# Three head pairs with float32 PV instead of four, scaled weight parts on a third engine, and an order planned with other durations

## The chip, the cores and the metric

The kernel runs on one core of a Trainium2 chip. The metric is the device time of one execution in microseconds (us), lower is better. Engines are named as the profile names them: PE (matrix products), PEld (its weight loads, which overlap PE), DVE, ACT and POOL (element-wise work), SP (the queue that issues most DMAs). The kernel is one program: each engine has its own list of instructions in a fixed order, and they wait for each other by semaphores.

## The reference, cut

Three layers over a batch of 4, 576 positions, 8 heads of 64 columns (model width 512), all float32:

```python
scores = (q @ k.T) / 8                       # per batch and head, 576 x 576
thresh = max(scores, axis=-1) - tau
attn   = exp(where(scores >= thresh, scores, -1e9) - max(scores))
x = (attn / sum(attn)) @ v                   # heads side by side: 576 x 512
x = x + relu(layernorm(x) * g @ w_ch1) @ w_ch2            # hidden width 2048
theta = x @ w_theta
y = w_tok_r @ (x * cos(theta)) + w_tok_i @ (x * sin(theta))
u = x + y
out = u + relu(u @ w_ch)
```

The kernel gives float32 accuracy from 16-bit matrix products by splitting each operand into a high and a low fp16 part and adding three products.

## The kernel before, in words

**Attention** goes by batch `b`, by tile `t` of 128 query rows (four full tiles and one tail of 64 rows per batch) and by head pair `hp` (0 to 3): one call of `couple(b, t, hp)` (L900) makes two units, one per head (the tail makes one). A unit's scores `S` are a product of 64 contraction rows (L930); DVE takes the row maximum and copies to `ringE` (`top`, L1037), ACT masks (L1053). From here there are two ways:

- *Whole* (`turned`, L992; pairs in `WHOLE`, L37: all four head pairs of batch 0): PE turns the masked scores with five float32 transposes per unit (`tm` L1008, `tl` L1009), ACT takes the exponential from PSUM (L1013, and L1021 for the tails of the pair), and the product with V (`pv`, L945) is float32. V is loaded as it is (`vraw`, L790) and nothing is split.
- *Split* (the end of `unit`, L1026, for all other pairs): ACT takes the exponential in place (L1079), `hi16` copies to fp16 on ACT, DVE or POOL (L305, L307 or L309), `lo16` and `lo16t` subtract on DVE or POOL (L318), and an SP DMA transposes the 16-bit tile (`PT<-ringP`, L1100). The product (L953 for batches 0 and 1, L958 for 2 and 3) has 14 fp16 instructions per unit and head. V needs its own split: a sum of squares on ACT (L813), one small product on PE (`pvs`, L820), scale steps, a high part on ACT (L838), a low part on DVE or POOL (L842 or L845).

**The first channel layer** goes by groups of three tiles (`ln_group`, L1160): layer norm, then per chunk of 128 hidden columns 12 products of 384 columns (`p_A`, L713) and 9 of 512 (`chA`, L736). Chunks 0 to 11 are made in three `Quad`s of eight weight pieces while attention runs; batch 0 has no such work until its first three tiles are done.

**Weights** arrive as 64-bit words (pairs of 32-bit) and `cvt` (L474) turns each piece into two fp16 parts: absolute value `s1` on ACT or DVE (L500, L502), low words `s1b` on ACT (L507), three DVE steps `s2a`, `s2b`, `s2c` (L511, L518, L523), an integer sum `s3` on POOL (L528), the scaled high part `s4` on ACT (L533) and the scaled low part `s5` on DVE (L539).

**The end**: `mix` (`y`, L1876) and `chan` (`o`, L1934) per batch; `chan`'s last steps per block of 128 output columns are two ACT halves (L1951), two DVE halves (L1958) and one output DMA (L1963).

**The order** is planned when the program is built. Every step is given to `Plan.op` with the engines that may do it and a duration in ns for each. `Plan.play` simulates the list of free engines: at each turn the step that can start first is placed, on the engine that would end it first. PE breaks ties by a key (attention before layer work), the others by the latest time at which the step may end, which `Plan.latest` works out backwards from the pass before. `LAT` stands for the way from one engine to another, `DMA_LAT` for a transfer's landing. `Plan.run` makes eight passes, keeps the ranks of the shortest and plays it for real. Where the plan leaves PE idle over 200 ns, `keep` (L460) puts in filling products (`warm<-one`, L466); the program starts with 20 products on ones (`warmup`, L458).

Of the kernel before, what the change touches and what calls it, by code (L numbers as in the profile page):

```python
# [22 lines left out]
KB = 4  # L23
# [12 lines left out]
WARM = 20  # L36
WHOLE = ((0, 0), (0, 1), (0, 2), (0, 3))  # L37
TRT = 580.0
PVT = 2250.0
# [15 lines left out]
LAT = 300.0  # L55
# [8 lines left out]
DMA_LAT = 2600.0  # L64
# [29 lines left out]
OFF = {"ln": -20000.0, "lnev": -10000.0, "cvt1": 0.0, "top": -500.0, "mask": -500.0, "exp": -5000.0, "thr": -2500.0, "hi16": 500.0, "lo16": -1500.0, "evict": -4000.0, "guard": -3000.0, "att": -1500.0, "prep": 0.0, "ev": -2500.0, "fill": -3000.0, "cvt": 6000.0, "late": LATE}  # L94

# [19 lines left out]
class Op:  # L115
    __slots__ = ("kind", "start", "pen", "fn", "engs", "deps", "acq", "rel", "key", "off", "grow", "first", "rank", "prev", "left", "users",
                 "ready", "fin", "eng")


class Plan:  # L120
# [5 lines left out]
    def op(self, fn, deps=(), acq=(), rel=(), key=0.0, kind="fill", pen=None, **engs):  # L126
        o = Op()
        o.pen = pen or {}
# [22 lines left out]
    def run(self, passes=8):  # L151
# [8 lines left out]
        best = rank = None  # L160
        for k in range(passes + 1):
            for res, was in free.items():
                res.free[:] = was
                res.last = {}
            for sl, n in uses:
                sl.uses, sl.i, sl.end = n, None, 0.0
            if k == passes:
                for o, r in zip(self.ops, best[1]):
                    o.rank = r
            span = self.play(k == passes)  # L170
            if k == passes:
# [28 lines left out]
    def play(self, real):  # L200
# [9 lines left out]
        while left:  # L210
# [40 lines left out]
            o.fin = clock[e] + (DMA_LAT if e == "Q" else 0.0)  # L251
# [25 lines left out]
def tile_kernel(  # L277
# [169 lines left out]
    k_load = op(c_load, A=100, kind="att")  # L447
# [26 lines left out]
    def cvt(src, shape, hi, lo, name, start=(), acq=(), kind="cvt", peak=None, late=None, early=False):  # L474
# [56 lines left out]
        def s4(e):  # L531
            if late:
                A.activation(out=hi(), in_=st["w"], func=AF.Copy, scale=late())  # L533
# [3 lines left out]
        def s5(e):  # L537
            if late:
                V.scalar_tensor_tensor(out=lo(), in0=st["w"], scalar=late(), in1=hi(), op0=ALU.mult, op1=ALU.subtract)  # L539
            else:  # L540
# [5 lines left out]
        ob = op(s1b, [o], A=ac(n), **kw)  # L546
# [318 lines left out]
    class Queries:  # L865


        def __init__(self, b, t, prev):
# [6 lines left out]
            def load_f(e):  # L875
                q["f"] = ap.tile([128, 4, 128], F32, tag=str(self.sl), name="qf_" + nm)
                Q.dma_start(q["f"], qT[b, :, :, c0:c0 + 128].rearrange("h p c -> p h c"))
# [15 lines left out]
            if b in QF:  # L893
                self.ready = [op(load_f, prev, (self.sl,), Q=1000, kind=kd)]
# [1023 lines left out]
    def chan(b):  # L1918
# [3 lines left out]
        for c in range(KB):  # L1922
# [15 lines left out]
            o = None  # L1938
            for kk in range(KB):
                o = op(mm(kk), [o, d["c"][kk], cw_ops[kk]] + pz_ops[b // 2][1:], sl if kk == 0 else (), T=6 * mh_(288),  # L1940
                       key=key + 0.01 * c)

            o_pre = o.deps[0]
# [22 lines left out]
            oa = [op(relu_(n), [o, o_p], (), (sl[n],), A=ap_(288), kind="ev") for n in range(2)]  # L1966
# [3 lines left out]
            op(out, oa, (), (sn,), Q=820)  # L1970
# [90 lines left out]
```

## Time and profile before

| what | us |
|---|---|
| median of 3 runs (lowest to highest) | 808.51 (808.27 to 809.12) |
| the profiled execution | 808.34 |
| its span, first to last instruction | 806.2 |
| PE busy in the span | 798.3 |
| DVE / ACT / POOL busy | 634.5 / 533.6 / 395.2 |

All rows are of that one execution. Times in rows count from the span's start. The duration of one PE instruction includes its way through the array, so consecutive products overlap: what a group occupies is read from its start to the start of the next group.

### The profile page before, as it was taken

How to read it: one execution, taken by the hardware profiler on the slowest of the kernel's cores; microseconds unless marked ns; L12 is line 12 of the kernel's file. 1: busy time of each engine (PE TensorE's matmuls, PEld its weight loads, DVE VectorE, ACT ScalarE, POOL GpSimd, SP SyncE). 2: the span in 40 equal slices, each digit the busy share in tenths (PEclk: the TensorE clock that was granted, in tenths of full speed). 3: DMA queues.
4: the chain of work that ended last, by engine and by line, in shares of the span. 5: the costliest groups of instructions: out<-in, count | busy, mean ns of one | idle time of the engine just before them, and what ended most of it. 6: DMA issues, size and time to landing. Idle time of an engine off the chain costs nothing.

```text
span 806.2 us, 16608 instructions
## 1 busy us (share of the span) xinstructions
PE 798.3 (99%) x6243; PEld 529.7 (66%) x6243; DVE 634.5 (79%) x1305; ACT 533.6 (66%) x980; POOL 395.2 (49%) x470
## 2 busy tenths in 40 slices
PE   9999999999999999999999999999999999999997
PEld 8888866665566677666655555555545777567775
DVE  4879799999789788888867777777668995698843
ACT  5899999997678788788835354455557461474612
POOL 1332478778577557687832122212354480545611
PEclk9999999999999999999999999999999999999999
DMA  8334598967387998968982532673374105010011
GB/s 230 136 101 137 180 201 185 214 143 126 108 160 158 155 199 175 218 124 147 159 209 115 173 98 76 236 244 131 89 173 140 32 21 105 1 60 1 16 45 59
DMA packets 194351, 106.40 MB, mean 132 GB/s; under 512 B 157408, under 2 KB 175328, under 8 KB 194272
## 3 DMA queue, kind: packets, MB, share of 16 engines
q1 hardware_dynamic: 193984, 105.34, 54.7%
q8 instruction: 49, 0.80, 0.4%
q14 instruction: 30, 0.25, 0.1%
q10 hardware_dynamic: 288, 0.00, 0.0%
HBM read 52.50 MB, written 15.73 MB: 85 GB/s over the span
## 4 chain that ended last, share of the span: by engine, by line
PE 92%; ACT 3%; DVE 2%; issue 1%; DMA 1%; POOL 0%; DVEq 0%; POOLq 0%
PE p_A L713 17%; PE chA L736 16%; PE y L1876 13%; PE S L930 9%; PE p_B L713 6%; PE c L736 6%; PE th L1712 5%; PE o L1934 5%; PE pv L945 4%; PE pv L958 4%; PE tm L1008 2%; PE pv L953 2%; PE warm L458 1%; DMA vraw<-in_v 1%; PE th_t L1712 1%
## 5 line engine op out<-in xcount | busy, mean ns | idle before, releaser
L713 PEld LDWEIGHTS <-w 128*128 128x128 f16 x1152 | 109.5, 98 | 78.0 <-issue 4.5
L736 PE MATMUL chA<-w,hbuf 128*128 128x512 f16 x648 | 149.5, 379 | 0.0
L713 PE MATMUL p_A<-ringX,w 128*128 128x384 f16 x864 | 148.7, 326 | 0.1
L736 PEld LDWEIGHTS <-hbuf 128*128 128x128 f16 x864 | 81.3, 98 | 92.0 <-issue 4.0
L1037 DVE TENSOR_SCALAR_CACHE_REDUCE ringE<-S,ncoef 128x576 f32<-128x576 f32 x144 | 112.7, 811 | 24.2 <-PE S L930 21.1
L318 POOL TENSOR_TENSOR ringP<-ringE,ringP 128x512 f16<-128x512 f32 (+2 forms) x118 | 123.0, 1056 | 13.5 <-ACT ringP L305 8.6
L1053 ACT ACTIVATE ringE<-ringE,tiny 128x576 f32<-128x576 f32 x144 | 105.6, 771 | 2.1 <-POOL tiny L1045 1.2
L1876 PE MATMUL y<-tok,z 128*128 128x288 f16 x768 | 97.4, 286 | 0.0
L1876 PEld LDWEIGHTS <-z 128*128 128x128 f16 x768 | 75.1, 98 | 19.4
L1079 ACT ACTIVATE ringE<-ringE,ntaup 128x576 f32<-128x576 f32 x108 | 78.4, 764 | 0.1
L309 POOL TENSOR_SCALAR ringP<-ringE 128x576 f16<-128x576 f32 x64 | 47.7, 748 | 41.1 <-ACT ringE L1079 39.3
L719 ACT ACTIVATE hbuf<-p_A 128x384 f16<-128x384 f32 x72 | 34.9, 485 | 49.4 <-PE p_A L713 48.9
L722 DVE SCALAR_TENSOR_TENSOR hbuf<-p_A,hbuf 128x384 f16<-128x384 f32 x72 | 39.3, 551 | 17.8 <-ACT hbuf L719 17.5
L1298 DVE SCALAR_TENSOR_TENSOR x<-chA,qs,x 128x512 f32<-128x512 f32 x54 | 40.0, 745 | 14.9 <-PE chA L736 13.6
L736 PE MATMUL c<-w,hbuf 128*128 128x512 f16 x216 | 50.7, 379 | 0.0
L713 PE MATMUL p_B<-ringX,w 128*128 128x384 f16 x288 | 50.6, 326 | 0.0
L930 PE MATMUL S<-kf,qf 64*128 64x288 f32 (+1 forms) x288 | 50.0, 426 | 0.1
L1934 PE MATMUL o<-x1T,cw 128*128 128x288 f16 x384 | 47.7, 286 | 0.0
L1934 PEld LDWEIGHTS <-cw 128*128 128x128 f16 x384 | 37.6, 98 | 9.7
L1712 PE MATMUL th<-th,x1T 128*128 128x512 f16 x192 | 42.6, 379 | 0.0
L313 ACT ACTIVATE x1T<-u,cs 128x576 f16<-128x576 f32 x16 | 12.3, 770 | 45.6 <-DVE u L1903 40.9
L528 POOL TENSOR_TENSOR raw_w<-raw_w 128x512 int32<-128x512 int32 x20 | 21.3, 1068 | 41.4 <-DVE raw_w L523 16.8
(243 smaller groups left out, 1568.9 us busy)
## 6 DMA issues: line engine op xcount, KB each, us to landing
raw_w<-in_w SPq DMA_DIRECT2D x20, 512.0 KB, 5.0
rawe<-in_w SPq DMA_DIRECT2D x12, 512.0 KB, 5.1
raw_tok<-in_wtok SPq DMA_DIRECT2D x12, 432.0 KB, 4.2
xscr<-x SPq DMA_DIRECT2D x18, 256.0 KB, 3.4
xl<-xscr SPq DMA_DIRECT2D x18, 256.0 KB, 4.9
out<-uo SPq DMA_DIRECT2D x16, 288.0 KB, 2.1
vraw<-in_v SPq DMA_DIRECT2D x12, 320.0 KB, 3.7
scr<-ringX SPq DMA_DIRECT2D x5, 768.0 KB, 5.0
```

What stands on the lines that cost most here:

```text
L309: G.tensor_scalar(out=out, in0=in_, scalar1=1.0, scalar2=0.0, op0=ALU.mult, op1=ALU.add)
L318: e.tensor_tensor(out=out, in0=a, in1=b, op=ALU.subtract)
L713: T.matmul(st["ps"][:, :n], lhsT=ch.w1(a, c), rhs=xt()[:, c, bb, :n], start=(kk == 0), stop=(kk == 11))
L736: T.matmul(ps, lhsT=h[:, a, t * 128:(t + 1) * 128], rhs=ch.w2(bb), start=(first and (a, bb) == M2[0]), stop=(stop and (a, bb) == M2[2]))
L930: T.matmul(w["S"][:, n, 0:288], lhsT=qd.q[a][r, hp], rhs=d.k[c][r, n * 288:(n + 1) * 288], start=(k == 0), stop=(k == len(seq) - 1))
L1037: V.tensor_scalar(out=st["e"].rearrange("p (a k) -> p a k", a=2), in0=st["S"][:, :, 0:288], scalar1=ncoef, scalar2=None, op0=ALU.mult, op1 ...
L1053: A.activation(out=st["e"], in_=st["e"], func=AF.Prelu, bias=cp["thr"][:, j:j + 1], scale=-1.0, alpha=STEEP)
L1079: A.activation(out=e_of(ws), in_=e_of(ws), func=AF.Exp, bias=ntaup, scale=1.0)
L1298: V.scalar_tensor_tensor(out=x[p, t0 + t], in0=st["ch", t], scalar=chunks[i].quad.inv, in1=x[p, t0 + t], op0=ALU.mult, op1=ALU.add)
L1712: T.matmul(st["ps"], lhsT=src(a, c), rhs=w[:, c * 512:(c + 1) * 512], start=(kk == 0), stop=(kk == 11))
L1876: T.matmul(st["ps"][n][:, 0:288], lhsT=a, rhs=w[:, n * 288:(n + 1) * 288], start=(k == 0 and q == 0), stop=(k == 8 and q == 2))
L1934: T.matmul(st["ps"][n][:, 0:288], lhsT=w[:, cs], rhs=d["t"][a][:, kk, n * 288:(n + 1) * 288], start=(kk == 0 and q == 0), stop=(kk == 3 an ...
```

## The change

1. `WHOLE` loses (0, 3): the fourth head pair of batch 0 goes the split way, with fp16 PV.
2. `s1b`, `s4` and `s5` of a weight piece may also go to POOL (`s5` as two instructions there).
3. The plan looks each step's duration up in a table `DUR` by engine, step and old duration; `LAT` is 180 instead of 300, `DMA_LAT` 2700 instead of 2600; `run` takes the fourth pass instead of the best of eight.
4. The start: 11 warming products instead of 20; the first queries' load is issued from ACT's queue instead of SP's.
5. The end: in the last block of the last batch the two column halves are computed one after the other and each has an output DMA of its own.

```diff
-WARM = 20
-WHOLE = ((0, 0), (0, 1), (0, 2), (0, 3))
+WARM = 11
+WHOLE = ((0, 0), (0, 1), (0, 2))
+S5G = 2000.0
-LAT = 300.0
+LAT = 180.0
-DMA_LAT = 2600.0
+DMA_LAT = 2700.0
+PICK = 3
+DUR = {
+    "T": {
...
+        "couple.pv": {850: 829, 950: 846, 2250: 2181},
+        "turned.tr": {580: 551},
+        "warmup": {4000: 6007},
...
+    "A": {
+        "cvt.s4": {550: 601, 617: 682},
+        "unit.expo.go": {760: 704},
+        "unit.mask": {760: 691},
...
-    def op(self, fn, deps=(), acq=(), rel=(), key=0.0, kind="fill", pen=None, **engs):
+    def op(self, fn, deps=(), acq=(), rel=(), key=0.0, kind="fill", pen=None, lat=0.0, **engs):
...
+        name = fn.__qualname__.replace("tile_kernel.<locals>.", "").replace("<locals>.", "")
+        engs = {e: DUR.get(e, {}).get(name, {}).get(round(ns), ns) for e, ns in engs.items()}
...
-    def run(self, passes=8):
+    def run(self):
...
-        for k in range(passes + 1):
+        rank = None
+        for k in range(PICK + 1):
...
-            span = self.play(k == passes)
-            if k == passes:
-                break
-            if best is None or span < best[0]:
-                best = span, [o.rank for o in self.ops]
+            span = self.play(k == PICK)
...
-    k_load = op(c_load, A=100, kind="att")
+    k_load = op(c_load, A=900, kind="att")
...
         def s1b(e):
             rw = st["rw"]
-            A.activation(out=rw[:, :, 0], in_=rw[:, :, 0].bitcast(U32), func=AF.Copy, scale=2.0 ** -29)
+            if e is A:
+                A.activation(out=rw[:, :, 0], in_=rw[:, :, 0].bitcast(U32), func=AF.Copy, scale=2.0 ** -29)
+            else:
+                G.tensor_scalar(out=rw[:, :, 0], in0=rw[:, :, 0].bitcast(U32), scalar1=2.0 ** -29, scalar2=0.0, op0=ALU.mult,
+                                op1=ALU.add)
...
+                    G.tensor_scalar(out=hi(), in0=st["w"], scalar1=late(), scalar2=0.0, op0=ALU.mult, op1=ALU.add)
...
+            elif late:
+                G.tensor_scalar(out=st["w"], in0=st["w"], scalar1=late(), scalar2=0.0, op0=ALU.mult, op1=ALU.add)
+                sub(G, lo(), st["w"], hi())
...
-        ob = op(s1b, [o], A=ac(n), **kw)
+        ob = op(s1b, [o], A=ac(n), G=CHG[1], **kw)
...
-            o_ = op(s4, [o] + deps, A=ac(n), **kw)
+            o_ = op(s4, [o] + deps, A=ac(n), G=CHG[1], **kw)
             if late:
-                return op(s5, [o_], (), [sl], V=vc(n, V2), **kw)
+                return op(s5, [o_], (), [sl], V=vc(n, V2), G=S5G, **kw)
...
-                self.ready = [op(load_f, prev, (self.sl,), Q=1000, kind=kd)]
+                self.ready = [op(load_f, prev, (self.sl,), Q=1000, kind=kd) if queries else
+                              op(load_f, (), (self.sl,), A=450, lat=3200.0, kind="guard")]
...
+            final = (b, c) == (B - 1, KB - 1)
...
+            if final:
+                for n in range(2):
+                    for kk in range(KB):
+                        o = op(mm1(kk, n), [o, d["c"][kk], cw_ops[kk]] + pz_ops[b // 2][1:], (sl[n],) if kk == 0 else (),
+                               T=3 * mh_(288), key=key + 0.01 * c)
+                    by_n.append(o)
...
+                        Q.dma_start(outT[b, c * 128:(c + 1) * 128, ns], st["u"][:, 0, ns])
```

## Rows read from the trace of the kernel before

**Rows 1.** The page, section 1: busy time, share of the span, instructions.

```profile
PE 798.3 (99%) x6243; PEld 529.7 (66%) x6243; DVE 634.5 (79%) x1305; ACT 533.6 (66%) x980; POOL 395.2 (49%) x470
```

**Rows 2.** What PE waited for: total us, times, longest us.

```profile
PE pvs L820 <- ACT va L813: 1.3, 2, 1.1
```

**Rows 3.** Filling products, lines by form, before 97 us and whole (times, busy, mean).

```profile
L466 PE MATMUL warm<-one 128*128 128x256 bf16 x37 | 5.9, 274 | 0.0
...
L466 PE MATMUL warm<-one 128*128 128x256 bf16 x52 | 7.9, 274 | 0.0
```

**Rows 4.** Two stretches: stretch, its us, PE, PEld, DVE, ACT, POOL busy, clock, DMA.

```profile
14.00:97.00 83.00, 82.75 (x699) 72.46 (x698) 68.53 (x180) 77.67 (x152) 26.86 (x35) 1.00 0.49 148
110.00:200.00 90.00, 89.61 (x844) 54.99 (x842) 88.54 (x193) 80.91 (x151) 73.25 (x82) 1.00 0.85 165
```

**Rows 5.** Timeline of PE, whole way: start, length, instruction; full pair, then tail.

```profile
76.33 0.66 PE L1008 MATMUL tm<-ident,ringE 128*128 128x128 f32 x4
...
76.93 1.00 PE L945 MATMUL pv<-vraw,PT 128*128 128x65 f32 x8
...
79.11 0.17 PE L611 MATMUL pw_w<-tiny,one 128*128 128x1 bf16 x1
...
94.20 0.68 PE L945 MATMUL pv<-vraw,PT 128*64 128x65 f32 x8
...
95.42 0.63 PE L945 MATMUL pv<-vraw,PT 128*64 128x65 f32 x8
```

**Rows 6.** Timeline of PE, split way of batch 1: one full pair, and what follows.

```profile
129.68 1.01 PE L953 MATMUL pv<-va,PT 128*128 128x65 f16 x28
130.52 0.81 PE L736 MATMUL chA<-w,hbuf 128*128 128x512 f16 x3
```

**Rows 7.** The start: timelines of PE to 4.98 and 8.5 us, of SP's queue.

```profile
0.98 4.27 PE L458 MATMUL warm<-ones 128*128 128x128 f32 x23 [0.98 <-POOL ones L424]
...
7.29 1.24 PE L930 MATMUL S<-kf,qf 64*128 64x288 f32 x8
...
0.72 0.40 SPq L757 DMA_DIRECT2D kf<-in_kT  x1
1.18 0.43 SPq L877 DMA_DIRECT2D qf<-in_qT  x1
```

**Rows 8.** Landing of the first query load, in us after its issue.

```profile
DMA to landing us min/median/max: 5.0/5.0/5.0
```

**Rows 9.** The end: timeline of ACT and DVE after 800 us.

```profile
801.39 0.89 ACT L1951 ACTIVATE uo<-o,cs 128x288 f32<-128x288 f32 x2 [2.13 <-PE o L1934]
801.98 0.95 DVE L1958 SCALAR_TENSOR_TENSOR uo<-uo,cs 128x288 f32<-128x288 f32 x2 [2.08 <-issue]
```

**Rows 10.** Lines by form, whole span: the split way's steps on POOL and ACT.

```profile
L318 POOL TENSOR_TENSOR ringP<-ringE,ringP 128x512 f16<-128x512 f32 x78 | 98.0, 1261 | 6.5 <-ACT ringP L305 4.2
L309 POOL TENSOR_SCALAR ringP<-ringE 128x576 f16<-128x576 f32 x64 | 47.7, 748 | 41.1 <-ACT ringE L1079 39.3
L318 POOL TENSOR_TENSOR ringP<-ringE,ringP 128x128 f16<-128x128 f32 x33 | 23.5, 712 | 6.6 <-ACT ringP L305 4.0 <-DVE ringP L307 2.0
...
L1079 ACT ACTIVATE ringE<-ringE,ntaup 128x576 f32<-128x576 f32 x108 | 78.4, 764 | 0.1
```

**Rows 11.** Lines by form, 0 to 97 us: weight pieces on ACT and DVE.

```profile
L533 ACT ACTIVATE w<-raw_w,qs 128x512 f16<-128x512 f32 x8 | 5.9, 795 | 0.0
...
L539 DVE SCALAR_TENSOR_TENSOR w<-raw_w,qs,w 128x512 f16<-128x512 f32 x8 | 6.2, 801 | 0.6 <-ACT w L533 0.6
L518 DVE TENSOR_SCALAR a_w<-a_w 128x512 uint32<-128x512 uint32 x14 | 6.2, 442 | 0.1
L523 DVE SCALAR_TENSOR_TENSOR rawe<-rawe,a_w 128x512 uint32<-128x512 uint32 x6 | 4.1, 676 | 0.0
```

**Rows 12.** Two DVE lines, 100 to 200 us: ns shortest/median/longest, first and last start.

```profile
L518 DVE TENSOR_SCALAR a_w<-a_w x10: 408/737/1376, 108.0 to 196.3; 128x512 uint32<-128x512 uint32 x10
...
L523 DVE SCALAR_TENSOR_TENSOR rawe<-rawe,a_w x6: 683/978/1173, 112.8 to 197.3; 128x512 uint32<-128x512 uint32 x6
```

More of the change, by code (lines that the diff above doesn't have):

```diff
@@ L250, in play @@
             before, clock[e] = clock[e], s + o.engs[e]
-            o.fin = clock[e] + (DMA_LAT if e == "Q" else 0.0)
+            o.fin = clock[e] + (DMA_LAT if e == "Q" else o.lat)
             o.eng, o.start = e, s
@@ L532, in s4 @@
             if late:
-                A.activation(out=hi(), in_=st["w"], func=AF.Copy, scale=late())
+                if e is A:
+                    A.activation(out=hi(), in_=st["w"], func=AF.Copy, scale=late())
+                else:
+                    G.tensor_scalar(out=hi(), in0=st["w"], scalar1=late(), scalar2=0.0, op0=ALU.mult, op1=ALU.add)
             else:
@@ L537, in s5 @@
         def s5(e):
-            if late:
+            if late and e is V:
                 V.scalar_tensor_tensor(out=lo(), in0=st["w"], scalar=late(), in1=hi(), op0=ALU.mult, op1=ALU.subtract)
+            elif late:
+                G.tensor_scalar(out=st["w"], in0=st["w"], scalar1=late(), scalar2=0.0, op0=ALU.mult, op1=ALU.add)
+                sub(G, lo(), st["w"], hi())
             else:
@@ L1936, in mm, with mm1, go @@
                 return go
[L1938 to L1943, printed above, removed]
+            final = (b, c) == (B - 1, KB - 1)
+            def mm1(kk, n, c=c, sl=sl, st=st):
+                def go(e):
+                    if kk == 0:
+                        st.setdefault("ps", []).append(m_tile(sl[n], [128, 512], f"o_{b}_{c}_{n}"))
+                    cs = slice(kk * 512 + c * 128, kk * 512 + (c + 1) * 128)
+                    for q, (w, a) in enumerate(((cw(0), 0), (cw(0), 1), (cw(1), 0))):
+                        T.matmul(st["ps"][n][:, 0:288], lhsT=w[:, cs], rhs=d["t"][a][:, kk, n * 288:(n + 1) * 288],
+                                 start=(kk == 0 and q == 0), stop=(kk == 3 and q == 2))
+                return go
+            o, by_n = None, []
+            if final:
[4 more added lines that the diff above has]
+                    by_n.append(o)
+            else:
+                for kk in range(KB):
+                    o = op(mm(kk), [o, d["c"][kk], cw_ops[kk]] + pz_ops[b // 2][1:], sl if kk == 0 else (), T=6 * mh_(288),
+                           key=key + 0.01 * c)
+                by_n = [o, o]
+            o_pre = by_n[0].deps[0]
             def pre(e, c=c, st=st, sn=sn):
@@ L1965, in chan @@
             o_p = op(pre, [o_pre, d["c"][c]], [sn], V=vc(576, V2), G=gc(576), kind="ev")
-            oa = [op(relu_(n), [o, o_p], (), (sl[n],), A=ap_(288), kind="ev") for n in range(2)]
+            oa = [op(relu_(n), [by_n[n], o_p], (), (sl[n],), A=ap_(288), kind="ev") for n in range(2)]
             oa = [op(fin_(n), [oa[n]], V=vc(288), kind="ev") for n in range(2)]
@@ L1969, in chan, with half, go @@
             ends.append(o_p)
-            op(out, oa, (), (sn,), Q=820)
+            if final:
+                sn.uses = 2
+                def half(n, c=c, st=st):
+                    def go(e):
+                        ns = slice(n * 288, (n + 1) * 288)
+                        Q.dma_start(outT[b, c * 128:(c + 1) * 128, ns], st["u"][:, 0, ns])
+                    return go
+                for n in range(2):
+                    op(half(n), [oa[n]], (), (sn,), Q=820)
+            else:
+                op(out, oa, (), (sn,), Q=820)
         op(lambda e: None, ends, (), (d["sl"],), C=0)
```

163 lines of the change are left out of this document (156 added, 7 removed).

## The prediction

> **What bounds the kernel now.** The page comes first: PE is busy for 798.3 of 806.2 us [rows 1]. Busy PE may hide waits, so I read next who PE waited for: the longest entry is 1.3 us in all [rows 2]. The timeline shows that groups follow each other without gaps, so PE's own work sets the end almost everywhere. Two parts of that work are useless: the warming products, which occupy the time from 0.98 us to the first scores at 7.29 us with two fills [rows 7], and the fills, 52 in all, 37 of them before 97 us [rows 3]. Their busy time of 5.9 and 7.9 us [rows 3] includes the way through the array; by 256 columns at 2.4 GHz (the granted clock is 1.00 [rows 4]) a fill occupies 0.11 us, an estimate: 37 are 4.1 us, 52 are 5.7 us.
>
> Then the stretches [rows 4]. From 14 to 97 us, while batch 0's attention runs alone, the other engines have room: DVE 68.5, ACT 77.7 and POOL 26.9 us of 83 each, together 173.1 of 249, or 70%. From 110 to 200 us, with layer work beside attention, they have little: 88.5, 80.9 and 73.3 of 90 each, 90% together, and DVE is at 98%. A reader should keep both in mind: a microsecond taken off PE is worth a microsecond only as long as these three keep up.
>
> The sums below go against the profiled execution, 808.34 us (span 806.2 and 2.1 around it); the median of the runs is 808.51.
>
> **The fourth head pair on the split way.** Removed on PE for a full pair: two units of transposes, 0.60 us each (76.33 to 76.93), and the float32 product, 2.18 us (76.93 to 79.11) [rows 5]: 3.38 us. Added: 28 fp16 products in 0.84 us (129.68 to 130.52) [rows 6]. Scores are the same. That is 2.5 us per pair and four full pairs: 10.2 us. The tail pair loses 0.60 and 1.22 us (94.20 to 95.42) [rows 5] and gains about 0.9: 0.9 us saved. Together 11.1 us less. PE gets one more `pvs` product, and in an in-order engine its wait for ACT's sum of squares can show: it cost up to 1.1 us once [rows 2]. Bounds 0 and 1.1, I take 0.3, since the list puts most of these products where their input is long there.
>
> What it adds elsewhere: POOL gets nine copies of 748 ns, nine subtractions of 1261 ns and, per pair, a tail step of 712 ns (five) [rows 10]: 6.7 + 11.3 + 3.6 = 21.6 us. ACT is about even (an exponential of 764 ns per unit [rows 10] for the one it had from PSUM, one step for the tails less, three short ones for V more). DVE gets about 1 us of V's low part. SP gets nine transposing DMAs; the stretch from 14 to 97 us has a DMA share of 0.49, against 0.85 in the next one [rows 4], so I cost them at nothing; behind each one, waiting in SP's queue for POOL's subtraction, the next weight and query loads stand; if those were late, PE would lack chunks, and that is priced with the crowding below.
>
> **Scaled weight parts on POOL.** This is a means, not a gain on PE. A piece's `s4` costs ACT 795 ns and its `s5` costs DVE 801 ns [rows 11]; POOL's nearest rows are 748 ns for a copy, and that plus 1261 for the two-step `s5` [rows 10], so about 2.0 us. The plan chooses. If the first stretch shrinks by 11.1 us, its load is (173.1 + 22) of 3 x 71.9, or 90%: exactly the density of the stretch from 110 to 200 us, and only if POOL takes most of the addition.
>
> What does 90% cost? The later stretch shows it: 15 fills after 97 us (52 less 37 [rows 3]), 1.7 us, and even if all lie in these 90 us PE is otherwise fed. In the first stretch no layer work can stand in, and it has 37 fills already. I take 1.7 us of new idle time; the bounds are minus 5.7 us (every fill reclaimed by a better order) and plus 4.1 us (as many early fills again).
>
> **The start.** The warming ends some 2 us sooner: 23 of its 40 records (two per product) have started by 4.98 us [rows 7], so 22 end about there. What is late next is data. The first query load is issued at 1.18 us [rows 7] and lands 5.0 us later [rows 8], at 6.2 us. Issued from ACT's queue it can go at 0.72 us, as the key load does [rows 7], or behind the two small loads of `c_load`, near 1.6 us: it lands at 5.7 to 6.6 us. Scores then start 0.7 to 1.6 us earlier than 7.29. I take 1.2; bounds 0 (PE runs into the next loads) and 2.0. The Trainium skill speaks against more: by "Trainium Kernel Development and Optimization", Key Constraints, DMAs of several queues share the same 16 engines and issuing from another saves only issue time. By that the second queue is worth 0.46 us (1.18 - 0.72), the rest being the shorter warming; no run shows a large load issued by ACT.
>
> **The end.** Now both halves wait for the last product: ACT's two take 0.89 us from 801.39, DVE's two end at 802.93 [rows 9]. Computed in turn, only the second half is left, about 0.45 + 0.5 us: 0.55 us sooner, and its DMA carries half the bytes. I take 0.7; bounds 0.3 and 1.3. PE's products and weight loads are as many as before.
>
> **The new plan.** Durations, LAT and the pass change the order everywhere. PE is at 99% of the span [rows 1], so outside the first stretch a new order has little to gain: beyond the fills, bounds are 0 and 3 us lost (an estimate: twice the longest entry of PE's waits [rows 2], rounded up). I take 0, because this changes which step is next, not how much work stands ready.
>
> Sum: 808.34 - 11.1 + 0.3 + 1.7 - 1.2 - 0.7 = **797.3 us**, with its own range of 793.5 to 801.5.
>
> **Rival 1: fills reclaimed as well.** If the order with read durations also fills the holes, the 1.7 us of new idle time falls away and the 52 fills, 5.7 us, turn into work: 797.3 - 1.7 - 5.7 = 789.9 us. For it: the guessed order left 37 fills in a stretch where no engine was above 94%. Against: the same stretch will be at 90%, and in the later one that density had holes too.
>
> **Rival 2: the gain given back to the three engines.** If DVE's two-input steps are as slow beside a busy POOL from the start as they are between 110 and 200 us, a piece costs DVE more: `s2b` 737 ns for 442, `s2c` 978 for 676 [rows 11, 12], 0.6 us per piece. Fourteen pieces (the count of `s2b` before 97 us [rows 11]) make 8.3 us: DVE then needs 68.5 + 1 + 8.3 = 77.8 us in the first stretch, at its best rate of 98% 79.4 us, where PE would need 71.9. PE's 11.1 us shrink to 3.6: 808.34 - 3.6 + 0.3 - 1.9 = 803.1 us. Against: `s5` may leave DVE, 0.8 us for each piece.
>
> **Rival 3, slower: DVE blocked by POOL.** The same place, but each of `s1`, `s2b`, `s2c` and `s5` on DVE is held for part of a POOL step. It decides from about 1.0 us per piece: then the first stretch takes DVE 68.5 + 1 + 14 = 83.5 us of work, 85 us at 98%, and the start's and end's 1.9 us are eaten. At 1.4 us per piece it needs 89.1, 90.5 us at 98%: 808.34 + 7.5 + 0.3 - 1.9 = 814.2 us. For it: `s2b` took up to 1376 ns where its shortest was 408 [rows 12], and POOL's load in this stretch nearly doubles. Against: the medians are far from the longest. The Trainium skill ("SBUF — State Buffer", Who interferes with whom) has DVE and POOL share one port pair as an exclusive lock: a DVE step in a two-port mode or with two SBUF inputs and a POOL step fully block each other. The trace agrees in kind, 408 against 1376 ns for one step.
>
> **Rival 4: it doesn't do what it says.** If the plan left `s1b`, `s4` and `s5` on ACT and DVE, ACT (77.7 us in a stretch of 72) would hold the first stretch at 77.7 / 0.98 = 79 us: about 803 us, as in rival 2 and counted with it.
>
> **How the numbers follow.** Forecast 0.56, rival 1 0.15, rivals 2 and 4 together 0.17 (801.5 to 808), rival 3 0.12. A measurement of this kernel tells about 0.2% from no change, 1.6 us. All of the forecast and of rival 1 is faster by more, and 0.13 of the 0.17, the other 0.04 lying within 0.2%; rival 3 gives 0.10 slower and 0.02 within. So faster 0.84, same 0.06, slower 0.10. The range runs from 789.5 (nearly half of rival 1 lies below) to 806.5 (rivals 2 and 4 but for their worst); it leaves out 0.06 below and 0.13 above.
>
> **What would show it.** Right: batch 0's attention over ten or more us earlier; a quarter fewer float32 `pv` records; `s4` and `s5` rows on POOL; about 40 to 60 fills and few PE waits; first scores near 6.1 us; one ACT and one DVE half after the last product. Wrong: PE waits of several us on `hbuf`, `ringE` or weight parts between 85 and 200 us; `s2b` near 0.7 us before 85 us (rival 2) or its kin over 1 us (rival 3); first scores not before 7 us; new gaps after 200 us, for which I allowed nothing.

## The result and the profile after

The changed kernel takes 819.7 us (815.67 to 822.04, four runs) against 808.73 us beside it: the ratio is 1.0127, 95% interval 1.0110 to 1.0144. It is slower by 11 us; I forecast 797.3. The profiled execution took 822.04 us with a span of 820.2; it lies at the slow end of the four, so sums go against spans.

The page, sections 1 and 2 (busy time of each engine; granted clock of PE in 40 slices, tenths):

```profile
PE 801.2 (98%) x6206; PEld 522.1 (64%) x6206; DVE 658.6 (80%) x1318; ACT 507.5 (62%) x933; POOL 454.2 (55%) x540
...
PEclk9999989999999999999999999999999999989999
```

PE is busy *longer* than in [rows 1], with 37 instructions fewer; in two slices the clock is low. The stretches of [rows 4] and those between (columns as there, the last but one before DMA share being the clock):

```profile
0.00:14.00 14.00, 10.39 (x62) 8.60 (x62) 3.35 (x14) 6.20 (x10) 3.41 (x22) 1.00 0.84 235
14.00:97.00 83.00, 81.37 (x699) 67.49 (x699) 75.45 (x184) 70.48 (x140) 57.62 (x73) 0.96 0.62 164
97.00:110.00 13.00, 10.84 (x90) 7.12 (x90) 10.61 (x26) 10.36 (x19) 11.79 (x17) 0.82 0.73 187
110.00:200.00 90.00, 89.57 (x847) 53.73 (x847) 85.42 (x183) 74.61 (x140) 72.48 (x83) 0.99 0.86 175
200.00:640.00 440.00, 437.63 (x3225) 258.43 (x3224) 359.78 (x755) 271.62 (x500) 241.29 (x298) 1.00 0.64 153
640.00:800.00 160.00, 154.96 (x1157) 113.82 (x1156) 116.83 (x152) 69.30 (x118) 65.07 (x48) 0.98 0.12 35
```

Three things stand here: PE is idle for 3.6 us before 14 us and for 2.2 us from 97 to 110 us (1.0 in each before), the clock is below 1.00 in four stretches, and PE is idle for 5 us after 640 us, where no attention is left. What PE waited for (total us, times, longest):

```profile
PE pvs L989 <- ACT va L982: 2.4, 2, 1.4
PE o L2104 <- DVE x1T L2079: 2.3, 2, 1.2
PE S L1100 <- DVE ringE L1207: 2.1, 3, 1.4
PE pt L1834 <- DVE r_t L1900: 2.0, 1, 2.0
PE ptr L1410 <- ACT xn L1382: 1.7, 1, 1.7
```

Where before the longest line had 1.3 us [rows 2], five lines make 10.5 us. The waits that lie before a fall of the clock, and one more in the last such stretch, on PE's timeline (start, length, instruction, wait before it):

```profile
8.72 0.16 PE L989 MATMUL pvs<-tiny,one 128*128 128x1 bf16 x1 [1.38 <-ACT va L982]
14.13 1.97 PE L1100 MATMUL S<-kf,qf 64*128 64x288 f32 x8 [1.39 <-DVE ringE L1207]
104.47 0.66 PE L1410 MATMUL ptr<-ident,xn 128*128 128x128 f32 x4 [1.73 <-ACT xn L1382]
725.29 0.66 PE L1834 MATMUL pt<-ident,xl 128*128 128x128 f32 x4 [1.98 <-DVE r_t L1900]
727.47 1.44 PE L1882 MATMUL th<-th,x1T 128*128 128x512 f16 x3 [0.73 <-DVE x1T L1856]
```

and the three stretches of 6.8 us, which begin 2.4 us after the start that ended the wait at 14.13, 0.8 after 104.47 and 1.2 after 725.29 (columns as above):

```profile
16.50:23.30 6.80, 6.80 (x32) 6.23 (x33) 4.44 (x10) 3.96 (x10) 3.38 (x4) 0.50 0.29 95
105.30:112.10 6.80, 6.80 (x44) 3.90 (x44) 5.72 (x15) 5.95 (x12) 5.74 (x9) 0.50 1.13 203
726.50:733.30 6.80, 6.07 (x16) 2.02 (x14) 6.80 (x13) 4.99 (x9) 3.63 (x2) 0.50 0.24 89
```

In all three PE ran at 1.2 GHz, at 0.50. In the first two its busy time is full all the same, and in the third only the wait of 0.73 us is missing: the lower clock hides in the busy share. Before has no such stretch after its start.

To see where time went, I added up PE's instructions from each one's start to the next one's start, took the waiting apart, and set down separately what the lower clock added (half of the PE time inside a stretch at 0.50). Spans of the profiled executions in us; "turns" are `tm` and `tl`, "layers" the products of all weights:

| | before | after | w4_old | w3_old | w4_new | fill | nodur | only_t |
|---|---|---|---|---|---|---|---|---|
| float32 `pv` + turns + fp16 `pv` | 114.8 | 103.9 | 115.7 | 105.3 | 116.0 | 104.3 | 105.5 | 104.9 |
| layers | 576.2 | 577.7 | 576.4 | 576.0 | 576.7 | 578.3 | 576.6 | 577.5 |
| scores | 86.1 | 90.7 | 89.2 | 89.6 | 89.6 | 90.1 | 89.4 | 88.2 |
| fills | 6.4 | 4.7 | 2.8 | 9.8 | 3.1 | 9.6 | 11.2 | 11.4 |
| warming | 6.0 | 5.0 | 4.7 | 5.0 | 4.5 | 5.0 | 5.1 | 4.8 |
| idle | 2.0 | 14.3 | 4.6 | 8.2 | 14.3 | 7.5 | 8.1 | 15.1 |
| lower clock | 0 | 9.9 | 0 | 4.8 | 5.1 | 1.7 | 0 | 0 |
| after PE's last start | 5.2 | 4.1 | 4.0 | 4.0 | 4.0 | 4.1 | 4.1 | 4.3 |
| rest | 9.5 | 9.9 | 9.9 | 9.9 | 10.1 | 14.5 | 9.9 | 9.9 |
| span | 806.2 | 820.2 | 807.3 | 812.6 | 823.4 | 815.1 | 809.9 | 816.1 |

From before to after the attention products save 10.9 us and the end 1.1; idle time takes 12.3, the lower clock 9.9, the scores 4.6 (groups of scores that start one product at a time, each waiting for a free buffer, count as scores; in `fill` about 5 us of the rest are products put into the steps' own buffers). Milestones agree: the first `p_A`, which follows batch 0's first three tiles, starts 1.3 us *later* than before, the 216th 5.3 later (206.5 for 201.2), the last 6.9 (504.9 for 498.0), the last `o` 15.1 (816.1 for 801.1).

### The profile page after: what moved, and what is told of

Same layout as the page of the kernel before. It is cut to its first block, busy times and chain, and to the rows that moved or that the text cites. A ratio compares the mean times of both kernels' runs of the same rounds, so it can differ in the third digit from the quotient of the medians.

```text
span 820.2 us, 16615 instructions
## 1 busy us (share of the span) xinstructions
PE 801.2 (98%) x6206; PEld 522.1 (64%) x6206; DVE 658.6 (80%) x1318; ACT 507.5 (62%) x933; POOL 454.2 (55%) x540
## 4 chain that ended last, share of the span: by engine, by line
PE 72%; DVE 7%; issue 1%; POOL 1%; ACT 1%; DMA 0%; SPq 0%; DVEq 0%; POOLq 0%
PE chA L905 15%; PE p_A L882 13%; PE y L2046 13%; PE p_B L882 6%; PE c L905 6%; PE th L1882 5%; PE S L1100 5%; PE pv L1128 4%; PE o L2104 3%; PE pv L1123 1%; PE th_t L1882 1%; DVE uo L2148 1%; DVE r L1969 1%; DVE w L705 1%; DVE ringE L1207 1%
## 5 line engine op out<-in xcount | busy, mean ns | idle before, releaser
L882 PE MATMUL p_A<-ringX,w 128*128 128x384 f16 x864 | 151.7, 328 | 0.4 <-DVE hbuf L891 0.3
L477 POOL TENSOR_TENSOR ringP<-ringE,ringP 128x512 f16<-128x512 f32 (+2 forms) x108 | 104.7, 977 | 22.5 <-ACT ringP L464 17.0
L1249 ACT ACTIVATE ringE<-ringE,ntaup 128x576 f32<-128x576 f32 x117 | 85.3, 764 | 0.1
L477 DVE TENSOR_TENSOR ringP<-ringE,ringP 128x512 f16<-128x512 f32 (+2 forms) x74 | 56.2, 767 | 7.2 <-ACT ringP L464 4.1
L1100 PE MATMUL S<-kf,qf 64*128 64x288 f32 (+1 forms) x288 | 56.3, 442 | 2.2 <-DVE ringE L1207 2.1
L468 POOL TENSOR_SCALAR ringP<-ringE 128x576 f16<-128x576 f32 x53 | 38.7, 731 | 30.2 <-ACT ringE L1249 28.8
L2104 PE MATMUL o<-x1T,cw 128*128 128x288 f16 x360 | 45.1, 286 | 2.3 <-DVE x1T L2079 2.3
L1882 PE MATMUL th<-th,x1T 128*128 128x512 f16 x192 | 45.3, 397 | 0.7 <-DVE x1T L1856 0.7
L2104 PEld LDWEIGHTS <-cw 128*128 128x128 f16 x360 | 35.2, 98 | 11.7 <-issue 2.7
```

Of the source, the lines that this page charges most:

```text
L477: e.tensor_tensor(out=out, in0=a, in1=b, op=ALU.subtract)
L882: T.matmul(st["ps"][:, :n], lhsT=ch.w1(a, c), rhs=xt()[:, c, bb, :n], start=(kk == 0), stop=(kk == 11))
L1100: T.matmul(w["S"][:, n, 0:288], lhsT=qd.q[a][r, hp], rhs=d.k[c][r, n * 288:(n + 1) * 288], start=(k == 0), stop=(k == len(seq) - 1))
L1249: A.activation(out=e_of(ws), in_=e_of(ws), func=AF.Exp, bias=ntaup, scale=1.0)
L1882: T.matmul(st["ps"], lhsT=src(a, c), rhs=w[:, c * 512:(c + 1) * 512], start=(kk == 0), stop=(kk == 11))
L2104: T.matmul(st["ps"][n][:, 0:288], lhsT=w[:, cs], rhs=d["t"][a][:, kk, n * 288:(n + 1) * 288], start=(kk == 0 and q == 0), stop=(kk == 3 an ...
```

## The experiments

Eighteen kernels; times are medians, beside a kernel before of 808.7 to 809.4 us. "Old plan" is the plan of before: guessed durations, LAT 300, DMA_LAT 2600, best of eight passes. Three theories stood at first: the clock and the waits are the loss; the fourth split pair is, since three engines lack room or its chain is longer; the new plan is.

### Which part of the change costs

`w3_old`, the change with the old plan; `before_w3`, before with the one line alone; `w4_new`, the change without that line; `w4_old`, all of the change but the pair and the plan:

```diff
# w3_old (against the change): also the best of eight passes again; w4_old: also the fourth pair in WHOLE
-DUR = {...}
+DUR = {}
-LAT = 180.0
+LAT = 300.0
-DMA_LAT = 2700.0
+DMA_LAT = 2600.0
...
# before_w3 (against before); w4_new is the reverse, against the change
-WHOLE = ((0, 0), (0, 1), (0, 2), (0, 3))
+WHOLE = ((0, 0), (0, 1), (0, 2))
```

> The changed kernel with the plan of before (no duration table, LAT 300, DMA_LAT 2600, the best of eight passes); three float32 head pairs, the POOL forms of the weight steps, the start and the end are kept. If the tight plan is the cause (its steps come later on the chip than planned, so PE meets inputs that are not there), PE waits are back at a few us, the clock stays at 1.00 and the 11 us of PE work show: 796 to 802. If the three other engines have no room for the fourth pair's split whatever the plan, waits or fills take the 11 us: 806 to 812.

> The kernel before with one edit: three float32 head pairs instead of four. If PE's work decides, about 808.5 - 11 = 798. If ACT, DVE and POOL have no room without the weight steps' POOL forms, fills replace the work and it is 805 to 812; its row for fills then counts 50 to 100 more than the 52 of before.

> The changed kernel with four float32 head pairs as before; everything else of the change is kept, the new plan too. If the tight plan alone brings waits and the fallen clock, it is as slow as the changed kernel or slower: 815 to 828, clock under 0.995. If it is the split pair that crowds the engines, this one has room again: 803 to 808, clock 1.00.

> The changed kernel with four float32 pairs and the plan of before: what is left of the change are the POOL forms of the weight steps, the start and the end. If the tight plan is what made the run with four pairs and the new plan 824, this one is near the kernel before or a little under it: 804 to 809. If the POOL forms make it (POOL steps that block DVE, short steps queued behind long ones), it is 812 or more.

| | four float32 pairs | three |
|---|---|---|
| old plan, with POOL forms, start and end | 809.12 (1.0005, 0.9996 to 1.0014) | 812.83 (1.0047, 1.0032 to 1.0062) |
| new plan | 824.07 (1.0184, 1.0168 to 1.0200) | 819.7 (1.0127) |

The line alone gave 814.3 (1.0061, 1.0046 to 1.0076), above the range for either theory, with 41 more fills and not 50 to 100. So the POOL forms, start and end together change nothing; the pair costs 3.7 us under the old plan; and the new plan costs 15 us with four pairs and 7 with three. Under the new plan the pair does help, by 4.4 us, of the 12.1 that PE saves there (116.0 to 103.9). Each cell is one order, and `pick5` below moves the time by 4.8 us by its order alone, so 3.7 and 7 us are not sizes to carry elsewhere. That three pairs bring nothing with guessed durations rests on four orders: `before_w3`, `w3_old`, and `nodur` and `nodur300` below lie between 811.0 and 814.3 us.

### Is the clock a cause?

`fill` keeps the changed kernel's order and puts filling products ahead of nine of PE's waiting places, so that PE is not still there (`more` puts them ahead of the step, `INSIDE` names the steps in whose own buffer they go):

```diff
+EXTRA = {
+    ('Keys.__init__.total', 0): 12,
+    ('couple.qk.go', 2): 12,
...
+                    if (name, i) in EXTRA:
+                        if name in INSIDE:
+                            self.n = EXTRA[name, i]
+                        else:
+                            self.more(EXTRA[name, i], s)
                 o.fn(self.handles[e])
```

> The changed kernel in its own order, with filling products (each into a PSUM buffer that is free or that the next step owns) put on PE ahead of nine of the twelve places where it waited: 12 each ahead of the first V sum and the third scores, 15 ahead of the transpose at 104 us, 18 ahead of the one at 725 us, and so on. If the clock that fell to 1.2 GHz after such waits is the larger part of the loss (the granted clock was 0.987, three stretches of 6.8 us at half), it stays at 1.00 and the time falls by some 10 us, to 809 to 812. If the fallen clock is only a sign of waiting, which costs what it costs anyway, the time stays at 815 to 822 or grows by the fills (86 more, up to 9 us).

815.72 us (814.82 to 816.88; 1.0076, 1.0059 to 1.0093): 4 us faster than the change. The lower clock falls from 9.9 to 1.7 us; the one stretch that is left lies where the fills stand *behind* a wait, in the buffer that the step waits for:

```profile
719.76 2.56 PE L652 MATMUL pt<-one 128*128 128x256 bf16 x13 [1.96 <-DVE r_t L1932]
...
720.20:723.60 3.40, 3.40 (x18) 2.60 (x16) 3.40 (x7) 1.01 (x2) 0.96 (x1) 0.50 0.22 87
```

(PE's timeline, and a stretch.) So the clock is a cause on top of the waits: work that computes nothing made the kernel faster, though by less than the 10 us of the first theory, because the fills take PE time too (4.9 us more in the row of fills and about 5 in the steps' buffers).

The four executions of the change point the same way with no edit at all. They took 815.67, 818.01, 821.4 and 822.04 us at mean granted clocks of 0.994, 0.991, 0.987 and 0.987. The clock's missing share of each span (0.013 of 820.2 us is 10.7) leaves 808.8 to 809.5 us in all four, where the profiled execution of before has 806.2. By this estimate the clock makes 5 to 11 us of the loss and all else about 3. It is not the whole in every order: 6 us to before remain in `fill` with the clock nearly full, and the profiled execution of `only_t` below has none of it before its last product and takes 817.9 us.

### What the pair runs into under the old plan

`light_w3` and `light_w4` are before with three and four pairs, order unchanged, and without the steps `s1b`, `s2b`, `s2c` and `s3` of the 24 quad pieces:

```diff
         def s2b(e):
+            if light:
+                return
             a = st["a"]
```

> The same steps left out of the kernel before with three float32 head pairs (814.3 with them). If the fourth pair's split is slow because the three engines have no room for it before 210 us, room is there now and the 11 us of PE work show at least by half: 5 to 11 us below the run with four pairs, 797 to 803. If it is its order or its longer chain through POOL and the transposing DMA, it stays 3 to 6 us above the run with four pairs, 810 to 815.

> The kernel before in its own order, with four steps of each of the 24 weight pieces converted during attention left out (s1b, s2b, s2c and s3, so these weights are not the right ones): about 27 us of DVE, 17 us of ACT and 25 us of POOL fall away, all before 210 us. It is the base for the next run. If the kernel before is bound by PE, as its profile says, nothing changes: 806 to 809.5. If the three engines were its limit between 110 and 200 us, it is 3 to 8 us faster.

810.39 us (1.0017, 1.0008 to 1.0027) and 807.44 (0.9979, 0.9970 to 0.9988). From 14 to 97 us DVE, ACT and POOL have 71.9, 78.7 and 40.4 us of work in `before_w3` and 57.0, 74.8 and 25.8 in `light_w3`, 77 and 63% of the three; yet three pairs stay 3.0 us behind four (4.9 with all steps, 814.3 less 809.4). With the order fixed, room on the three engines is thus worth about 2 of the 15 us between PE's saving (9.8 us in `before_w3`) and the result. Of the 3.0 us some is clock: in six of its ten executions `light_w3` has a mean granted clock of 0.996 or 0.997, and the four at 1.000 take 808.9 to 809.5 us. What PE waits for in `light_w3`, and its longest wait for that DMA on the timeline:

```profile
PE pv L962 <- DMA PT<-ringP: 2.4, 3, 1.7
PE y L1885 <- ACT hbuf L305: 1.4, 1, 1.4
...
163.46 1.02 PE L962 MATMUL pv<-va,PT 128*128 128x65 f16 x28 [1.70 <-DMA PT<-ringP]
```

The first line is the split way (exponential, copy, subtraction, transposing DMA, product), but not the added pair's: 2.1 of the 2.4 us are at 157 and 163 us, in batch 1, which goes the split way in both kernels. The added pair's four full products start without any wait, and its tail after 0.25 us at most. The rest of the loss is in 93 fills (11.7 us; before has 52, 6.4 us) that this order has, because it was planned for the loaded engines. So the run does not show that their load is harmless: an order made for the lighter kernel was not tried.

`w3_nofill` and `e_nofill` leave out all fills after the first 16 us, from `before_w3` and from before with the split end; `before_e15` has the split end and 15 warming products:

```diff
-                if e == "T" and self.idle and s - before > IDLE:
+                if e == "T" and self.idle and s - before > IDLE and s < 16000.0:
```

> The kernel before with three float32 pairs (814.3) and no fills after 16 us, in the same order; it had 93, some 75 of them after 16 us. If those took PE time for nothing, 8 us come back: 806 to 808, and PE waits little more. If they stand where PE waits anyway, the waits grow by as much and it stays at 812 to 815. If the clock falls without them, 815 to 825.

> The kernel before in its own order with the change's end, and without the 35 filling products after 14 us. If fills after the start take PE time in which real work stood ready, the time falls by up to 35 x 0.11 = 3.9 us and by the end's 0.7: 804 to 806. If they lie only where PE would wait anyway, they turn into waits: 807.5 to 808.5. If they are what keeps the clock up, it falls somewhere and the time is 809 or more.

> The kernel before in its own order with the change's end (two halves, two output DMAs) and 15 warming products instead of 20. By the rows of before, 30 records end near 5.8 us, the first queries have landed at 6.2, so scores start 0.9 us sooner, and the end saves 0.7: 806.8 to 808.3. If the first scores only move the wait to the next loads, and the smaller DMA saves nothing, 808.5 to 809.5.

`w3_nofill` took 817.08 us (1.0129, 1.0074 to 1.0184), 2.8 more than with fills. Its profiled execution took 826.63 us, with a span of 824.7 for 812.7 in `before_w3`: there 9.6 us of fills turned into 6.9 us more idle time and 13.2 us more at the lower clock, in stretches such as

```profile
70.00:83.60 13.60, 12.95 (x78) 11.26 (x80) 8.90 (x19) 8.51 (x15) 2.71 (x3) 0.50 0.49 128
175.80:186.00 10.20, 10.04 (x75) 6.38 (x71) 10.20 (x21) 7.29 (x14) 8.06 (x10) 0.50 1.06 220
```

What PE stands before in batch 0's attention shows here too, since no fill covers it. Before 97 us PE waits four times ahead of scores, 3.6 us in all, until DVE has copied earlier scores out, and 1.2 us for ACT's mask:

```profile
30.02 1.97 PE L930 MATMUL S<-kf,qf 64*128 64x288 f32 x8 [1.35 <-DVE ringE L1037]
70.65 1.11 PE L1008 MATMUL tm<-ident,ringE 128*128 128x128 f32 x4 [1.16 <-ACT ringE L1053]
```

`e_nofill` took 807.47 us (0.9988, 0.9978 to 0.9997), the best kernel that computes everything, and `before_e15` 808.41 (0.9994, 0.9984 to 1.0004). In before a fill hides waits so short that nothing is lost without it; with three pairs the holes are real, and the fills in them keep the clock.

### What in the new plan costs

`lat300` and `w4_lat300` set LAT back; `nodur` empties the table of durations, `nodur300` does both; `pick5` takes the order of the fifth revision; `margin` has LAT 300 and makes the durations of ACT, DVE and POOL 8% longer; `only_t` uses the table for PE alone, `no_t` for the three others alone:

```diff
# pick5
-PICK = 3
+PICK = 5
# margin
-        engs = {e: DUR.get(e, {}).get(name, {}).get(round(ns), ns) for e, ns in engs.items()}
+        engs = {e: DUR.get(e, {}).get(name, {}).get(round(ns), ns) * (1.08 if e in "AVG" else 1.0) for e, ns in engs.items()}
# only_t (no_t: if e != "T")
+        engs = {e: DUR.get(e, {}).get(name, {}).get(round(ns), ns) if e == "T" else ns for e, ns in engs.items()}
```

> The changed kernel with one number back, LAT 300 instead of 180: the plan leaves 0.12 us more on every way between engines and gives 802 us for itself instead of 789. If the changed plan is slow because it has no margin (its steps come 9 us late at 100 us and 30 us late at the end), the waits fall from 14 us to under 9, the clock stays near 1.00 and the time is 807 to 814. If it is the durations or the choice of the pass, little changes: 816 to 822.

> The same number put back in the changed kernel with four float32 pairs (824): if the missing margin is the cause, 808 to 816, and under the run with three pairs as the plan of before had it; if not, 820 to 826.

> The changed kernel with the table of read durations emptied; LAT 180, DMA_LAT 2700, the third revised order and everything else stay. Between this kernel and the one with the whole old plan (812.83 us) only LAT, DMA_LAT and the choice of the pass remain. Theory 1 (the read durations cost the remaining 7 us: they are means read beside another order, so the list puts dependent steps too close): 813 us, between 811.5 and 814.5, PE idle near 8 us and no half-clock stretch after 200 us. Theory 2 (the margin LAT does it, durations or not): 818 us or more, PE idle above 11 us. Theory 3 (any new order of these steps scatters by several us): anything from 811 to 822, and then the other three runs of this set scatter as much without following margin or durations.

> The same with LAT 300 as well: guessed durations and the old margin; what still differs from the old plan is DMA_LAT 2700 for 2600 and that the third revised order is taken and not the shortest planned of eight. Theory 1 (durations): 813 us, as without LAT 300. Theory 2 (margin): 813 us too, 5 below the run with guessed durations and LAT 180. Theory 3 (scatter): 811 to 822. At 817 or more the choice of the pass or DMA_LAT would be left as the cause.

> The changed kernel with the order of its fifth revision in place of the third; durations, LAT and all steps are the same, and its planned span is 791.7 us against 789.3. It sizes how much the time depends on the order alone. Theory 3 (orders scatter): differs from 819.7 by more than 3 us either way. Theories 1 and 2: 819.7 give or take 3, with waits of more than 1 us on PE after 640 us again.

> The changed kernel with LAT 300 and with the planned durations of ACT, DVE and POOL 8% longer, so that the list leaves room for steps that run later than read. Theory 1 (durations too short for the order they lead to): 813 to 816 us, PE idle under 9 us, since the list then asks no more of the three engines than the old one did. Theory 2 (LAT alone): 819, as with LAT 300 alone. Theory 3: anything from 811 to 822. If it is slower than 819, too much room costs as well: more fills and more planned idle time (planned span 834 us).

> The changed kernel with the table of read durations used for PE alone; ACT, DVE and POOL are planned with the guesses, which are 5, 7 and 11% longer in sum (540.3, 700.5, 501.7 us for 513.2, 655.0, 452.5). LAT 180 and the pass as in the changed kernel. Theory A (the guesses for ACT, DVE and POOL are the reserve that the old order had): 813 us, as with the whole table emptied, PE idle near 8 us. Theory B (PE's own guesses, 1% longer in sum, are the reserve, since PE then runs ahead of the plan everywhere): 819 us. Theory C (only orders differ): neither this run nor the next follows the table.

> The reverse: the table is used for ACT, DVE and POOL, and PE is planned with the guesses (781.1 us of work for 772.6). Theory A: 819 us, give or take 3. Theory B: 813 us. Theory C: no relation to either.

| three pairs, new plan with | us | ratio, 95% | planned span | span of the profiled execution |
|---|---|---|---|---|
| nothing else (the change) | 819.7 | 1.0110 to 1.0144 | 789.3 | 820.2 |
| LAT 300 (`lat300`) | 819.15 | 1.0102 to 1.0135 | 802.4 | 817.8 |
| no table (`nodur`) | 813.06 | 1.0031 to 1.0067 | 808.6 | 809.9 |
| no table, LAT 300 (`nodur300`) | 811.04 | 1.0013 to 1.0036 | 816.2 | 809.3 |
| another order (`pick5`) | 814.89 | 1.0061 to 1.0102 | 791.7 | 816.5 |
| 8% longer, LAT 300 (`margin`) | 844.37 | 1.0407 to 1.0450 | 834.4 | 843.1 |
| table for PE alone (`only_t`) | 818.54 | 1.0104 to 1.0158 | 809.1 | 816.1 |
| table for the others alone (`no_t`) | 829.09 | 1.0235 to 1.0272 | 807.4 | 824.0 |

With four pairs LAT 300 gave 818.36 us (1.0116, 1.0101 to 1.0132), 5.7 less than `w4_new` and between the two ranges named for it; with three it gave nothing, and with the table empty 2.0 us, where the two intervals overlap. The planned span is the end of the last step in the simulation of free engines that fixes the order; before's was 818.2, and the chip took 806.2.

What follows. Emptying the table gives back 6.6 of the 7 us, as the theory said by which the read durations cost them. But that they are only too short is not borne out by `margin`: guesses and 8% more give the three engines nearly the same sums (ACT 551 and 557, DVE 696 and 701, POOL 496 and 496 us, `nodur300` and `margin`), and 811.0 and 844.4 us. Splitting the table also gave no half: each half alone is at or over the whole, 818.5 and 829.1. And with the table untouched, another revision of the order is 4.8 us faster. So eight orders of the same steps lie between 811 and 844 us, and the planned span does not rank them, except that `margin` is last in both: the change has the shortest planned span of the eight and is sixth, level with `lat300`. All of the six that use any of the table run behind their plan on the chip, by 7 to 31 us; before, `w4_old` (813.3 planned, 807.3), `w3_old` (814.4, 812.6) and `nodur300` run ahead of theirs, and `nodur` is on time.

`only_t` shows the waits of such an order with no fall of the clock:

```profile
PE pvs L989 <- ACT va L982: 3.2, 3, 1.7
PE th L1882 <- DVE x1T L1856: 2.6, 1, 2.6
PE ptr L1410 <- ACT ringE L1249: 1.7, 1, 1.7
```

## Why the prediction was wrong, point by point

**PE's work: right.** Minus 11.1 us forecast, minus 10.9 measured (table above; minus 10.4 between `w4_old` and `w3_old`). Lines by form show a quarter of the float32 products gone:

```profile
L1115 PE MATMUL pv<-vraw,PT 128*128 128x65 f32 x192 | 26.8, 285 | 0.0
L1115 PE MATMUL pv<-vraw,ringP 128*128 128x65 f32 x48 | 9.8, 287 | 0.0
...
L625 PE MATMUL warm<-one 128*128 128x256 bf16 x37 | 5.5, 273 | 0.0
```

Before they were 256 and 64.

**Crowding: the term that fell first.** I took 1.7 us, from the fills of the stretch at 90%, with a bound of plus 4.1. Between the spans of `w4_old` and `w3_old`, the pair alone, 7.0 us of fills and 3.6 of idle time eat the saving of 10.4, and 4.8 of the lower clock come on top: 15.4. The step that failed is reading a price of density off the *fills* of the later stretch. There PE has layer work to put between; in the first one it has none. From 14 to 97 us `w3_old` has 57 fills, 54 of them right ahead of scores, and `w4_old` has one; `w3_nofill` shows what is waited for there: DVE's copies of earlier scores. PE, with less work of its own between, comes to the next scores before DVE has made room for them. The split pair's own products are not what it stands before: in `w3_old` the four full ones have neither a wait nor a fill ahead of them. Whether less load on the engines would help in an order made for it is not shown. My bound of 4.1 was too small, and the whole saving of 11.1 would have been too: with the clock the pair took more than it gave.

**The new plan: the larger miss.** "I take 0, because this changes which step is next, not how much work stands ready", bounded by 3. It costs 7 us here and 15 with four pairs. The bound, "twice the longest entry of PE's waits", is none for a new order, for [rows 2] are the waits of an order that happened to fit. What such an order exposes can be seen at 102 us (POOL, then ACT, timelines):

```profile
99.26 1.75 POOL L477 TENSOR_TENSOR w<-raw_w,w 128x512 f16<-128x512 f32 x1
...
101.36 0.66 POOL L669 TENSOR_SCALAR rawe<-rawe 128x512 int32<-128x512 uint32 x1
102.10 0.80 POOL L1215 TENSOR_TENSOR tiny<-tiny,taup 128x1 f32<-128x1 f32 x1
...
102.93 0.78 ACT L1223 ACTIVATE ringE<-ringE,tiny 128x576 f32<-128x576 f32 x1 [2.45 <-POOL tiny L1215]
103.62 0.80 ACT L1382 ACTIVATE xn<-x,tiny 128x512 f32<-128x512 f32 x1
```

DVE's last row maxima before it end at 100.71 and 101.45 us; POOL's small step stands behind other steps, most of them weight steps that the change lets POOL do, until 102.10; ACT's mask waits 2.45 us for it, the layer norm's `xn` stands behind the mask on ACT, PE's `ptr` waits 1.73 us for that, and 0.8 us later the clock is at 0.50. From 97 to 110 us POOL, which has the new weight steps, is busy for 11.8 of 13 us, ACT and DVE for 10.4 and 10.6. So it is the place of single steps in the queues that makes the wait, and on POOL there is little room besides.

**The clock: not in the sum at all.** I used 1.00 throughout, since [rows 4] show it, and made it no rival. In the profiled run it is 9.9 us, nearly as much as PE's saving. It comes with either of the two terms above: `w3_old` has 4.8 us of it, `w4_new` 5.1, `w4_old` none. The Trainium skill ("TensorE: Matmul & The Clock Gate", A second HAM failure mode: psum-queue depth-cycling) says that frequent short idle times between groups of products can make the clock swing between its levels; the trace agrees in kind, with three stretches that cost 9.9 us, but each came after only one or two waits of 1.4 to 2.0 us, not after frequent short ones. I had weighed neither.

**`pvs`: too low.** 0.3 us taken, 1.1 at most; measured are 2.4 in two waits for 1.3 before, 1.1 more, and the new one alone took 1.38. There are 13 such products for 12, and the one that the change adds is the first of all, at 8.72 us (before they begin at 94.1): the list put it at the head of batch 0, where nothing has been prepared, so the reason that I gave ("most of these products where their input is long there") failed for just this one.

**Start: right in size, and lost in this order.** First scores at 5.97 us (7.29 before), 1.3 sooner for 1.2. The queries' load went out at 0.71 us from ACT's queue and landed 4.3 us later, about 1.2 us sooner than before. By the rule of the Trainium skill ("Trainium Kernel Development and Optimization", Key Constraints) that another queue saves only issue time, the prediction had made it 0.46 us; the load landed 0.7 us faster as well, and no run shows why. But the next things were late: 1.38 us at 8.72, 1.39 at 14.13, and then the lower clock. The 32nd score product starts at 23.6 us for 18.4; with the same start and the old plan it is 17.3 (`w3_old`) and 17.7 (`w4_old`). `before_e15`, with ten records of warming fewer and the load still on SP, has its first scores at 7.17.

**End: right, 0.7 forecast.** After PE's last start 4.1 us are left for 5.2, and 4.5 in `before_e15` and `e_nofill`. One half of ACT and of DVE is left, for two each in [rows 9]:

```profile
816.46 0.50 ACT L2141 ACTIVATE uo<-o,cs 128x288 f32<-128x288 f32 x1 [0.92 <-PE o L2116]
816.99 0.52 DVE L2148 SCALAR_TENSOR_TENSOR uo<-uo,cs 128x288 f32<-128x288 f32 x1 [0.85 <-ACT uo L2141]
```

**The rivals.** Rival 3 had the sign, and 814.2 us, but its mechanism did not happen: from 14 to 97 us a piece's steps on DVE are held up little, where it needed 1.0 us per piece:

```profile
L681 DVE TENSOR_SCALAR a_w<-a_w 128x512 uint32<-128x512 uint32 x13 | 7.4, 567 | 0.1
L686 DVE SCALAR_TENSOR_TENSOR raw_w<-raw_w,a_w 128x512 uint32<-128x512 uint32 x8 | 5.9, 738 | 0.1
L686 DVE SCALAR_TENSOR_TENSOR rawe<-rawe,a_w 128x512 uint32<-128x512 uint32 x5 | 4.9, 985 | 0.0
```

`s2b` and `s2c` take 18.2 us for 13 pieces; in the same stretch before it was 16.8 (5.8, 6.9 and 4.1) for 13 `s2b` and 14 `s2c`, so about 0.2 us more per piece, and the seven `s5` left on DVE take 0.2 us more each. (The rival's own sum was off too: 89.1 / 0.98 is 90.9, not 90.5, which makes it 814.6 us.) Rival 2, the same in small, needed 0.6 us per piece and falls with it. Rival 1 is the opposite of what happened: fills went from 52 to 37, but into waits. Rival 4 falls: from 0 to 97 us POOL made 14 of the `s1b` and 7 of the `s4` steps. Of my signs of being right, batch 0's attention "over ten or more us earlier" and "few PE waits" failed; of those of being wrong, "new gaps after 200 us, for which I allowed nothing" is the one that was seen.

**What stays open**: which property of the planned order decides. The planned span does not, nor LAT, the table's halves or a common reserve; and how much of the 7 us is this one order's luck can't be told from eight orders. Open too is whether the pair could pay in an order in which DVE, ACT and POOL have room.

## What to carry to other kernels

When the limiting engine is at 99% of the span, its order happens to fit; a new order has to be measured, since here orders of the same steps spread over 33 us while the plan that promised most was sixth of eight. Work taken off that engine is worth its time only if the other engines make the inputs and buffers of its next step ready as much sooner; where no other work can stand in, the loss can be the whole saving and, with a fallen clock, more. Read the granted clock by short stretches beside every wait, and compare the executions of one kernel by it. Leave filling products where holes are real: without them `before_w3` was 2.8 us slower.

## What was unexpected of the hardware

- The clock fell to 1.2 GHz for 3.4 to 13.6 us at a time in runs whose PE was busy for 98% of the span (`w3_nofill` 805.1 of 824.7 us); in the change after single waits of 1.7 and 2.0 us or two of 1.4 us. It does not follow from the wait alone: in `only_t` PE waited 1.70 us at 8.71 us, the same place as in the change, and the clock stayed at 1.00 to the end; before's longest wait, 1.10 us at 97.85, left it too.
- The first record of the clock at 1.00 came between 3.8 and 6.9 us from the span's start, in kernels that begin with the same kind of warming products (`e_nofill` 3.84, before 4.03, `before_e15` 6.09, `fill` 6.80, `light_w4` 6.87); rows count the time before it as 1.00. In the change it came at 6.28, after the first scores had begun: their first two products took 642 and 639 ns, for 507 each before.
